# A small store of zeros goes onto the sync queue behind the first load

## The chip, the core and the metric

The kernel runs on one NeuronCore of a Trainium2 chip. The core has a matrix engine (TensorE, called PE in the profile), a vector engine (VectorE, DVE), a scalar engine (ScalarE, ACT), a general engine (GpSimd, POOL) and a sync engine (SyncE, SP) that here issues all transfers. Data lives in the off-chip memory (HBM) and is brought by DMA into the on-chip memory (SBUF), which has 128 partitions. A transfer is carried by 16 DMA engines.

The metric is the device time of one execution in microseconds (us): the median of 3 runs of the kernel before is 152.08 us, and the runs lie between 152.06 and 152.09.

## The reference

```python
B, S, D = 512, 32, 640          # x and fx: [512, 32, 640] bf16; alpha: [1] bf16

def reference(x, fx, alpha):
    return x + alpha * fx
```

So two tensors of 20.97 MB are read, one is written, and each element takes one multiplication and one addition. There is nothing to reuse.

## The kernel before

The three big tensors are seen as 128 rows of 80 x 1024 bf16 elements: one row for each SBUF partition (xv, fxv and ov, lines 59 to 61). A "column" below is a block of K = 1024 elements of every row, which is 256 KB over the 128 partitions. So x, fx and out have 80 columns each.

x is cut into three tiles (list X, line 18) of 32, 32 and 16 columns. The first of them is loaded by two transfers, of 4 columns and of 28 (X_CUTS, line 21). fx is cut into five tiles (list FX, line 19) of 16, 16, 19, 16 and 13 columns. Each x tile is overwritten in place with the result and then stored as a whole. Two x tiles and two fx tiles fit at a time (the pools "wide" and "fs", lines 66 and 67, with two buffers each), so a third load into a pool waits until the first tile has been used up: an x buffer is free when its store has landed, an fx buffer when the vector engine has read it.

Five helpers do the work: load_x (transfer on line 77), load_f (line 85), compute (one scalar_tensor_tensor on the vector engine, line 92, that computes fx * alpha + x over the columns that an fx tile and an x tile share), store (line 104) and alpha_to_lanes (lines 109 to 117). The last loads the single number alpha, spreads it over 128 partitions by a matrix product with a row of ones (line 115) and copies it to SBUF (line 117).

The order is written out by hand in the string PLAN (lines 22 to 41), and the schedule is manual: nothing reorders it. In PLAN "x 0" loads x tile 0, "f 1" loads fx tile 1, "c 2 1" computes fx tile 2 with x tile 1, "s 0" stores tile 0, and "a" fetches alpha. In the text below the transfers are called x0a (4 columns), x0b (28 columns), alpha, f0, f1, x1, f2, s0, f3, x2, f4, s1 and s2, which is the order in which SP issues them. All of them go on one queue, SP's, and SP issues strictly in this order: an instruction that waits on SP holds back all that follow. After the last store a no-op on SP waits for everything but that store (lines 126 to 129).

POOL runs nothing in this kernel apart from four small memsets of constants that the launch code puts ahead of the body (line 144).

Of the kernel before, what the change touches and what calls it, by code (L numbers as in the profile page):

```python
# [2 lines left out]

# [4 lines left out]

ACT = mybir.ActivationFunctionType
ALU = mybir.AluOpType  # L10
F32 = mybir.dt.float32
BF16 = mybir.dt.bfloat16

K = 1024
P = 128


X = [(0, 32), (32, 64), (64, 80)]
FX = [(0, 16), (16, 32), (32, 51), (51, 67), (67, 80)]

X_CUTS = {0: (4,)}
PLAN = """
x 0
a
f 0
f 1
x 1
c 0 0
f 2
c 1 0  # L30
s 0
f 3
x 2
c 2 1
f 4
c 3 1
c 3 2
s 1
c 4 2
s 2  # L40
"""


@with_exitstack
def kernel(
    ctx: ExitStack,
    tc: tile.TileContext,
    x: bass.AP,
    fx: bass.AP,
    alpha: bass.AP,  # L50
    out: bass.AP,
):

    nc = tc.nc
    xv = x.flatten_outer_dims().rearrange("(p n) d -> p (n d)", p=P)
    fxv = fx.flatten_outer_dims().rearrange("(p n) d -> p (n d)", p=P)  # L60
    ov = out.flatten_outer_dims().rearrange("(p n) d -> p (n d)", p=P)
    assert xv.shape[1] == X[-1][1] * K == FX[-1][1] * K

    consts = ctx.enter_context(tc.tile_pool(name="consts", bufs=1))
    psum = ctx.enter_context(tc.tile_pool(name="psum", bufs=1, space=bass.MemoryType.PSUM))
    wide = ctx.enter_context(tc.tile_pool(name="wide", bufs=2))
    fs = ctx.enter_context(tc.tile_pool(name="fs", bufs=2))
    ctx.enter_context(tc.manual_schedule())

    xt, ft = {}, {}  # L70
    done = []

    def load_x(i):
        a, b = X[i]
        xt[i] = wide.tile([P, max(e - s for s, e in X) * K], x.dtype, tag="x", name="x_t")
        for c, d in pairwise((a, *X_CUTS.get(i, ()), b)):
            r = nc.sync.dma_start(  # L77
                out=xt[i][:, (c - a) * K : (d - a) * K], in_=xv[:, c * K : d * K]
            )
            done.append(r)  # L80

    def load_f(j):
        a, b = FX[j]
        ft[j] = fs.tile([P, max(e - s for s, e in FX) * K], fx.dtype, tag="f", name="f_t")
        r = nc.sync.dma_start(out=ft[j][:, : (b - a) * K], in_=fxv[:, a * K : b * K])
        done.append(r)

    def compute(j, i):
        (fa, fb), (xa, xb) = FX[j], X[i]
        a, b = max(fa, xa), min(fb, xb)  # L90
        piece = xt[i][:, (a - xa) * K : (b - xa) * K]
        r = nc.vector.scalar_tensor_tensor(  # L92
            out=piece,
            in0=ft[j][:, (a - fa) * K : (b - fa) * K],
            scalar=lanes["a_f"][:],
            in1=piece,
            op0=ALU.mult,
            op1=ALU.add,
        )
        done.append(r)  # L100

    def store(i):
        a, b = X[i]
        r = nc.sync.dma_start(out=ov[:, a * K : b * K], in_=xt[i][:, : (b - a) * K])
        done.append(r)

    lanes = {}

    def alpha_to_lanes():
        a_1 = consts.tile([1, 1], alpha.dtype, name="a_1")  # L110
        done.append(nc.sync.dma_start(out=a_1[:], in_=alpha[None, :]))  # L111
        ones = consts.tile([1, P], alpha.dtype, name="ones")
        nc.vector.memset(ones[:], 1.0)  # L113
        a_ps = psum.tile([P, 1], F32, name="a_ps")
        done.append(nc.tensor.matmul(a_ps[:], ones[:], a_1[:], start=True, stop=True))  # L115
        lanes["a_f"] = consts.tile([P, 1], F32, name="a_f")
        nc.vector.tensor_copy(out=lanes["a_f"][:], in_=a_ps[:])  # L117

    does = {"x": load_x, "f": load_f, "c": compute, "s": store, "a": alpha_to_lanes}
    for step in PLAN.split("\n"):  # L120
        if step:
            what, *of = step.split()
            does[what](*map(int, of))


    rest = nc.sync.nop(nofuse=True)
    info = mybir.DependencyInfo(mybir.DependencyClass.Sync, mybir.DependencyReason.DATA)
    for i in done[:-1]:
        tc.add_manual_dep(rest.ins, i.ins.name, info, reason="all but the last store")


# [1 line left out]
_INS = ['x', 'fx', 'alpha']  # L133
_OUTS = [((512, 32, 640), 'bfloat16')]


# [23 lines left out]
```

## Time and profile before

| | |
|---|---|
| Median of 3 runs | 152.08 us (152.06 to 152.09) |
| The profiled execution: span from its first to its last instruction | 150.2 us |
| DMA share of the span (16 engines) | 98.1% |
| Bytes moved | 62.92 MB, at 419 GB/s over the span |
| Vector engine busy | 86.8 us, 58% of the span |
| Matrix engine busy | 0.2 us |
| POOL busy | 0.2 us, 4 memsets |

The profiled execution's own time is its span; no other time is given for it. The runs are 1.9 us longer than the span, which is what lies around the first and the last instruction.

How to read it. The page gives the busy time of each engine, the span in 40 slices, the DMA queues, and the chain of work that ended last, followed back from the end. A row "DMA f_t<-in_fx_dram" in this chain says that the chain ran through a transfer into an fx tile, from its issue on SP to its landing. Since transfers queue behind each other, most of such a time is spent in the queue. A list of the issues gives for each transfer its size and the time from issue to landing; where several transfers have the same size and line the median is given, and the view of one line gives the smallest, the median and the largest of its transfers. A landing is counted when the last of the 16 engines has reported.

### The profile page before, as it was taken

The numbers are of one execution on the slowest core, as the hardware profiler recorded it, in microseconds if no ns is written. First come the engines' busy times: TensorE is split into PE (matmuls) and PEld (weight loads), VectorE is DVE, ScalarE is ACT, GpSimd is POOL, SyncE is SP. The second block draws the span as 40 slices with busy tenths as digits, with TensorE's granted clock in tenths as the row PEclk, the third lists the DMA queues.
The fourth block names the chain that finished last, engine by engine and source line by source line (L and its number), as shares of the span: only waits on it lengthen the run. The fifth ranks groups of instructions, "written<-read, shape, count | busy, mean of one in ns | idle before, by whom it ended". The sixth has DMA issues, their size and how long they took to land.

```text
span 150.2 us, 78 instructions
## 1 busy us (share of the span) xinstructions
PE 0.2 (0%) x1; PEld 0.1 (0%) x1; DVE 86.8 (58%) x8; POOL 0.2 (0%) x4
## 2 busy tenths in 40 slices
PE   0000000000000000000000000000000000000000
PEld 0000000000000000000000000000000000000000
DVE  0000000049999999970399999106999999980000
POOL 0000000000000000000000000000000000000000
DMA  5997989999969696999696999999999969696994
GB/s 179 589 428 305 489 384 419 436 454 471 576 297 559 279 559 279 497 394 435 279 559 279 559 401 410 445 419 419 419 393 454 620 279 559 279 559 297 454 463 183
DMA packets 1730, 62.92 MB, mean 419 GB/s; under 512 B 194, under 2 KB 194, under 8 KB 194
## 3 DMA queue, kind: packets, MB, share of 16 engines
q1 hardware_dynamic: 1730, 62.92, 98.1%
HBM read 41.94 MB, written 20.97 MB: 419 GB/s over the span
## 4 chain that ended last, share of the span: by engine, by line
DMA 54%; DVE 35%; SPq 1%; issue 0%; DVEq 0%
DMA f_t<-in_fx_dram 54%; DVE x_t L92 35%; SPq L77 1%; SPq L111 0%; DVEq L92 0%
## 5 line engine op out<-in xcount | busy, mean ns | idle before, releaser
L92 DVE SCALAR_TENSOR_TENSOR x_t<-f_t,a_f,x_t 128x16384 bf16<-128x16384 bf16 (+3 forms) x6 | 86.5, 14438 | 25.5 <-DMA f_t<-in_fx_dram 25.5
L117 DVE COPY a_f<-a_ps 128x1 f32<-128x1 f32 x1 | 0.2, 159 | 21.5 <-PE a_ps L115 21.5
L113 DVE MEMSET ones<- 1x128 bf16 x1 | 0.2, 165 | 0.8 <-PEq L144 0.8
L115 PE MATMUL a_ps<-a,ones 1*128 1x1 bf16 x1 | 0.2, 158 | 22.2 <-DMA a<-in_alpha_dram 22.2
L144 POOL MEMSET const-bfloat16-1.0<- 128x1 bf16 x1 | 0.1, 103 | 0.0
L144 POOL MEMSET const-uint8-127<- 128x1 uint8 x1 | 0.1, 103 | 0.0
L115 PEld LDWEIGHTS <-ones 1*128 1x128 bf16 x1 | 0.1, 100 | 1.0 <-DVE ones L113 1.0
L144 POOL MEMSET const-float32-1.0<- 128x1 f32 x1 | 0.1, 100 | 0.0
L144 POOL MEMSET const-float32-0.0<- 128x1 f32 x1 | 0.1, 99 | 0.2 <-issue 0.2
## 6 DMA issues: line engine op xcount, KB each, us to landing
f_t<-in_fx_dram SPq DMA_DIRECT2D x3, 4096.0 KB, 35.6
x_t<-in_x_dram SPq DMA_DIRECT2D x1, 7168.0 KB, 21.3
f_t<-in_fx_dram SPq DMA_DIRECT2D x1, 4864.0 KB, 24.1
x_t<-in_x_dram SPq DMA_DIRECT2D x1, 4096.0 KB, 19.2
out_dram<-x_t SPq DMA_DIRECT2D x1, 4096.0 KB, 14.9
f_t<-in_fx_dram SPq DMA_DIRECT2D x1, 3328.0 KB
x_t<-in_x_dram SPq DMA_DIRECT2D x1, 1024.0 KB, 4.8
out_dram<-x_t SPq DMA_DIRECT2D x2, 24.7
```

What stands on the lines that cost most here:

```text
L77: r = nc.sync.dma_start(out=xt[i][:, (c - a) * K : (d - a) * K], in_=xv[:, c * K : d * K])
L92: r = nc.vector.scalar_tensor_tensor(out=piece, in0=ft[j][:, (a - fa) * K : (b - fa) * K], scalar=lanes["a_f"][:], in1=piece, op0=ALU.mult ...
L113: nc.vector.memset(ones[:], 1.0)
L115: done.append(nc.tensor.matmul(a_ps[:], ones[:], a_1[:], start=True, stop=True))
L117: nc.vector.tensor_copy(out=lanes["a_f"][:], in_=a_ps[:])
L144: nc = _bacc.Bacc("TRN2", target_bir_lowering=False, num_devices=1)
```

## The change

A tile named blank of 16 partitions by 512 bf16 elements (1 KiB per partition, 16 KiB in all) is set to zero by a memset on POOL at the start of the body. Right behind x0a, and ahead of x0b, SP issues a transfer that stores this tile to the first 512 elements of the first 16 rows of out. The store s0 later writes these places again with the result. s0 therefore waits for the small store too, and so does the no-op at the end, since the small store is in the list done. The wait of the small store for the memset is new on SP. On all engines the order of the other instructions is unchanged.

```diff
--- before.py
+++ after.py
@@ -18,6 +18,7 @@
 X = [(0, 32), (32, 64), (64, 80)]
 FX = [(0, 16), (16, 32), (32, 51), (51, 67), (67, 80)]
 
+HEAD = 16
 X_CUTS = {0: (4,)}
 PLAN = """
 x 0
@@ -67,6 +68,9 @@
     fs = ctx.enter_context(tc.tile_pool(name="fs", bufs=2))
     ctx.enter_context(tc.manual_schedule())
 
+    blank = consts.tile([HEAD, 512], out.dtype, name="blank")
+    nc.gpsimd.memset(blank[:], 0.0)
+
     xt, ft = {}, {}
     done = []
 
@@ -78,6 +82,8 @@
                 out=xt[i][:, (c - a) * K : (d - a) * K], in_=xv[:, c * K : d * K]
             )
             done.append(r)
+            if (i, c) == (0, 0):
+                done.append(nc.sync.dma_start(out=ov[:HEAD, :512], in_=blank[:]))
 
     def load_f(j):
         a, b = FX[j]
```

## The prediction

> **What bounds the kernel now.** I read the page's DMA part first, then the chain, then the list of issues, and last SP's own rows in the order of time. The DMA part settles who is the bound:
>
> ```profile
> span 150.2 us, 78 instructions
> q1 hardware_dynamic: 1730, 62.92, 98.1%
> HBM read 41.94 MB, written 20.97 MB: 419 GB/s over the span
> ```
>
> The 16 DMA engines are busy for 98.1% of the span, so the idle part is 1.9% of 150.2, or 2.9 us, and the start and the end take that. Any time that is won or lost is won or lost on the one queue that feeds these engines. The vector engine is busy for 58% only. The count of packets also says how a transfer is spread: 12 big transfers of 128 rows and 16 closing packets each are 12 x 144 = 1728, and alpha has 2.
>
> The question is then whether the queue runs equally fast everywhere. For that I take issue and landing times. The chain gives the landings of the fx tiles that the vector engine waited for:
>
> ```profile
> 1.16 0.42 SPq L77
> ...
> 1.99 30.16 DMA f_t<-in_fx_dram
> ...
> 49.59 24.12 DMA f_t<-in_fx_dram
> ...
> 94.31 26.12 DMA f_t<-in_fx_dram
> ```
>
> The row of L77 is SP's issue of x0b. In the DMA rows the first number is the issue, the sum is the landing: f0 lands at 32.15, f2 at 73.71, f4 at 120.43. The list of issues gives sizes and times to landing of the others, and the views of single lines give the largest and smallest of a line:
>
> ```profile
> x_t<-in_x_dram SPq DMA_DIRECT2D x1, 7168.0 KB, 21.3
> f_t<-in_fx_dram SPq DMA_DIRECT2D x1, 4864.0 KB, 24.1
> x_t<-in_x_dram SPq DMA_DIRECT2D x1, 4096.0 KB, 19.2
> x_t<-in_x_dram SPq DMA_DIRECT2D x1, 1024.0 KB, 4.8
> x_t<-in_x_dram SPq DMA_DIRECT2D x1, 58.3
> ...
> DMA to landing us min/median/max: 24.1/32.9/39.5
> ...
> DMA to landing us min/median/max: 14.9/22.8/26.6
> ```
>
> ```profile
> 0.73 0.86 SPq L77 DMA_DIRECT2D x_t<-in_x_dram  x2
> 1.63 0.32 SPq L111 DMA_DIRECT2D a<-in_alpha_dram  x1
> 1.99 0.87 SPq L85 DMA_DIRECT2D f_t<-in_fx_dram  x2
> 2.90 0.45 SPq L77 DMA_DIRECT2D x_t<-in_x_dram  x1
> 49.59 0.33 SPq L85 DMA_DIRECT2D f_t<-in_fx_dram  x1
> 66.78 0.35 SPq L104 DMA_DIRECT2D out_dram<-x_t  x1
> 67.19 0.42 SPq L85 DMA_DIRECT2D f_t<-in_fx_dram  x1
> 93.37 0.33 SPq L77 DMA_DIRECT2D x_t<-in_x_dram  x1
> ...
> 116.95 17.96 SPq L104 DMA_DIRECT2D out_dram<-x_t  x2
> ```
>
> With these, x0a lands at 0.73 + 4.8 = 5.5; x0b (issued at 1.16 by the chain) at 22.46; x1 at 2.90 + 58.3 = 61.2; s0 at 66.78 + 26.6 = 93.4; x2 at 93.37 + 19.2 = 112.57; s1, issued at 116.95, at 139.75 (the middle value, 22.8). The time from one landing to the next, per 1024 KB, is: x0b 16.9/7 = 2.42; f0 9.69/4 = 2.42; x1 (from f1, which is issued at about 2.43 and lands at 41.9) 19.3/8 = 2.41; **f2 12.51/4.75 = 2.63**; s0 19.66/8 = 2.46; f4 7.86/3.25 = 2.42; s1 19.32/8 = 2.41. So the queue runs at one steady rate, loads and stores alike, with one exception. f2, at 2.42, should take 11.50 us and takes 12.51: **1.0 us is missing**. No late issue explains it: f2 is issued at 49.59 and its place in the queue comes at 61.2. What happens during f2's turn is that SP issues the first store of the kernel, s0, at 66.78. The second store, s1, is issued at 116.95 in the middle of f4 in the same way, and f4 loses nothing (7.86 against 3.25 x 2.42 = 7.87). So the loss goes with the first store, not with stores as such.
>
> **The change part by part.** Five edits have to be priced.
>
> *The memset on POOL.* Lower end: the constants' memsets on POOL take 0.10 us each. Upper end: the vector engine's widest operation takes 20.485 us for 19456 elements a partition, 1.05 ns each, so 512 would take 0.54, with 0.10 on top 0.64 us. POOL has nothing else to do, and the body begins at about 0.8 (the first memset on DVE starts at 0.81). The zeros are there between 0.9 and 1.5 us. I take the upper end, as it is the nearer in width.
>
> *The issue on SP.* Issues take 0.32 to 0.45 us. SP is through with x0a at 1.10, then waits for the memset until 1.1 to 1.5, then issues for up to 0.45. x0b goes out at 1.5 to 2.0 instead of 1.16, and alpha, f0, f1 and x1, which are queued behind it on SP, go out 0.35 to 0.8 later. What hides this is x0a's own transfer. x0a takes 4.8 us from issue to landing, of which 2.42 are its bytes; the other 2.4 are start and close. If all of that were start, x0b would have to be issued by 5.5 - 2.4 = 3.1 us to be in the queue in time. It goes at 2.0 at the latest, so 1.1 us of cover is left and the cost is zero; without that cover each microsecond of delay would cost one. Alpha lands before 22.24 (the matmul on L115 starts then) and its result is first needed at 32.2, so its delay has 9.7 us of cover.
>
> *The bytes.* 16 KB at 2.42 us per 1024 KB are 0.04 us, plus a closing packet on each engine. Alpha's small transfer sits between x0b and f0, and f0 still shows 2.42 per 1024 KB, so a small transfer costs nothing that the landings show. I take 0.05, from 0.04 to 0.1.
>
> There is a rule that speaks against this edit: the Trainium skill, page "DMA: Bandwidth & Descriptors", section "Anatomy of one DMA — SWDGE (gpsimd) path", gives every transfer a fixed cost of about 2.0 us, most of it the wait for the write to be confirmed, and calls HBM the slowest target; the section states it for another queue than SP's. If that sat on the queue, the estimate from the page would be 152.08 + 2.0 = 154.1 us less whatever is won at f2. The closest row here is the turn from s0 to f3: f3 lands at 67.19 + 35.6 = 102.79 (35.6 is the median of f0, f1 and f3, and it is f3's), 9.4 us after s0 for 4 x 2.42 = 9.68, so f3 did not wait for s0's confirmation.
>
> *The first store is now another one.* In f2's turn the 1.0 us can go. By the landings' rounding (0.05 each) and the spread of the steady rate (2.41 to 2.44 times 4.75) the loss is 0.9 to 1.1; a landing is the last of 16 engines, and engines that came early may have lost more, so I keep 1.3 as the outer end. Below, it is 0 if the loss stays where it is. At the head the same loss may show up anew: 0 to 1.0 us. The trace has no store early on, so this is the open price. For 0: at that time the queue is still starting (2.4 us of x0a's 4.8 are not its bytes), so a delay of the first write can lie beside it; the store has one row for each of the 16 engines and 1 KiB in each, where s0 has 64 KiB rows; and all 16 are touched, so that s0 finds none for the first time. For 1.0: x0a and x0b are in flight as f2 was. I take 0, by the first ground, and keep 1.0 for the range.
>
> *The added waits.* s0 waits for the small store, which has landed some 60 us before; the no-op likewise. Both cost nothing, and would cost something only if the small store were later than 66 us. What is late next once f2 comes 1.0 us earlier? The vector engine starts f2's piece 1.0 earlier, f4's issue (94.31) and s1's (116.95) move along, and s1 is still issued 3.5 us before f4 lands, s2 (about 134.6) 5 us before s1 lands at 139.75. So the queue stays fed and all of the gain reaches the end.
>
> Sum: 0 + 0 + 0.05 - 1.0 + 0 + 0 = -0.95. Against the profiled span that is 150.2 to 149.25, and with the 1.9 us around it **151.1 us**, against the median of 152.08.
>
> **The rivals.** *The loss moves whole to the head.* If the first store stalls the queue for the same 1.0 us wherever it stands, x0b lands 1.0 later and f2 makes it good: 152.08 + 0.05 = 152.1. For it: the queue is busy in both places, and a busy queue has no gap for a stall. Against: the start is not yet at the steady rate.
>
> *The change does not do what it could: the loss is not the first store's.* f2 is also the one tile with 38 KiB rows, and f3 is issued right after s0, at 67.19. If the loss is f2's own or belongs to s0's large rows, nothing moves: again 152.1. Against: f4 has odd rows too (26 KiB) and keeps 2.42.
>
> *Slower: paid twice.* A first store stalls the queue at the head (1.0) and s0, the first large store, still stalls at f2 (1.0 as before): 152.08 + 1.0 + 0.05 = 153.1. It decides from the point where the head's stall exceeds what f2 gets back; with half a stall at the head it is 152.6. For it: the trace shows only that the second large store is free, not that a small one makes the first large one free. Against: only the argument that the small store touches all 16 engines and the same tensor.
>
> **How the numbers follow.** A measurement of this kernel can tell about 0.2%, 0.3 us, from no change. Forecast (stall gone from f2, most of it hidden at the head, 150.75 to 151.75): 0.60. Moved whole, or not the first store's at all, 152.1 for both: 0.07 and 0.06. Paid twice, 152.4 to 153.1: 0.27. Faster is the first case, same the second and third, slower the last. The range takes 150.8 (152.08 + 0.05 - 1.3) below, and above it goes to 152.8, which leaves the upper half of the slower case outside (0.13) and a few hundredths below. The forecast's own range is 150.8 to 151.75.
>
> **What would show it.** In the changed kernel's list of issues, f2's landing less x1's should be 11.5 us; if it is 12.5, the loss stayed. x0b's landing should be at 22.5 to 22.6; 23.5 says that the stall moved. SP's rows should show the small store's issue by 1.5 and x0b's by 2.0; x0b issued after 3.1 would open a gap in the first slices. The DMA share should stay at 98% or rise. Wrong I would be above all if a stall belongs to the first large write, or if the queue cannot hide a first write in its start.

## The result, and the profile after

The changed kernel takes 152.43 us (median of 20 runs, 152.03 to 153.81) against 152.06 us for the kernel before (20 runs, 151.90 to 152.25) on the same chip: a ratio of 1.0033, with an interval of 1.0018 to 1.0048. So it is slower, by 0.37 us, where 151.1 us and a gain were forecast. On two more chips it was slower by less: 152.03 against 151.95 us (1.0008, 0.9999 to 1.0017) and 152.09 against 151.95 us (1.0015, 1.0006 to 1.0024). Over the three, nothing is won, and 0.1 to 0.4 us are lost; on the second chip the interval still has room for no loss.

The profiled execution of the changed kernel took 152.44 us, with a span of 150.7 us. Its page:

```profile
span 150.7 us, 82 instructions
...
q1 hardware_dynamic: 1762, 62.93, 97.8%
HBM read 41.94 MB, written 20.99 MB: 418 GB/s over the span
...
L72 POOL MEMSET blank<- 16x512 bf16 x1 | 0.5, 514 | 0.3 <-POOLq L150 0.3
```

The packets are 32 more: 16 rows and 16 closing packets. The timeline shows what SP issues (start, time of the issue):

```profile
0.74 0.38 SPq L81 DMA_DIRECT2D x_t<-in_x_dram  x1
1.27 0.35 SPq L86 DMA_DIRECT2D out_dram<-blank  x1
1.67 0.41 SPq L81 DMA_DIRECT2D x_t<-in_x_dram  x1
2.13 0.32 SPq L117 DMA_DIRECT2D a<-in_alpha_dram  x1
2.50 0.82 SPq L91 DMA_DIRECT2D f_t<-in_fx_dram  x2
3.36 0.47 SPq L81 DMA_DIRECT2D x_t<-in_x_dram  x1
49.77 0.33 SPq L91 DMA_DIRECT2D f_t<-in_fx_dram  x1
66.97 0.34 SPq L110 DMA_DIRECT2D out_dram<-x_t  x1
67.37 0.44 SPq L91 DMA_DIRECT2D f_t<-in_fx_dram  x1
93.60 0.33 SPq L81 DMA_DIRECT2D x_t<-in_x_dram  x1
```

The list of issues (size, time from issue to landing), and the chain (issue, time to landing):

```profile
x_t<-in_x_dram SPq DMA_DIRECT2D x1, 7168.0 KB, 21.0
...
x_t<-in_x_dram SPq DMA_DIRECT2D x1, 4096.0 KB, 19.3
...
x_t<-in_x_dram SPq DMA_DIRECT2D x1, 1024.0 KB, 4.7
...
out_dram<-blank SPq DMA_DIRECT2D x1, 16.0 KB, 4.3
...
x_t<-in_x_dram SPq DMA_DIRECT2D x1, 58.0
```

```profile
2.50 29.85 DMA f_t<-in_fx_dram
...
49.77 24.44 DMA f_t<-in_fx_dram
...
94.82 26.02 DMA f_t<-in_fx_dram
```

| Landing, us | before | after | difference |
|---|---|---|---|
| x0a | 5.5 | 5.4 | |
| small store | | 5.6 | |
| x0b | 22.46 | 22.67 | 0.2 |
| f0 | 32.15 | 32.35 | 0.2 |
| x1 | 61.2 | 61.36 | 0.2 |
| f2 | 73.71 | 74.21 | 0.5 |
| f4 | 120.43 | 120.84 | 0.4 |

Two readings matter. x0b lands 0.2 us later, and f0 and x1 keep that distance. It can't be put down to the small store: over the thirteen traces of this case without a small transfer at the head, x0b lands between 22.5 and 22.8 us, and over the four with the small store between 22.6 and 22.8. Of the store's own cost the trace shows that its 16 rows took 0.046 us each. And f2 still stalls: it takes 74.21 - 61.36 = 12.85 us after x1's landing, where the steady rate gives 11.5. The stall has not gone and not moved; in this execution it is 0.3 us longer.

A shorter way to read the stall serves for the runs below. f2 is issued when the vector engine is done with f0, some 11.6 us before x1 lands, in all of these kernels. So the time from f2's issue to its landing is 11.6 plus f2's own turn: 24.12 before, 24.44 here, and about 23.15 where nothing stalls.

### The profile page after: what moved, and what is told of

The parts are those of the page before. It is cut to its first block, busy times and chain, and to the rows that moved or that the text cites. A ratio compares the mean times of both kernels' runs of the same rounds, so it can differ in the third digit from the quotient of the medians.

```text
span 150.7 us, 82 instructions
## 1 busy us (share of the span) xinstructions
PE 0.2 (0%) x1; PEld 0.1 (0%) x1; DVE 86.8 (58%) x8; POOL 0.7 (0%) x5
## 4 chain that ended last, share of the span: by engine, by line
DMA 53%; DVE 34%; SPq 1%; POOLq 0%; issue 0%; DVEq 0%
DMA f_t<-in_fx_dram 53%; DVE x_t L98 34%; POOLq L161 0%; SPq L81 0%; SPq L86 0%; SPq L117 0%; DVEq L98 0%; POOLq L150 0%
## 5 line engine op out<-in xcount | busy, mean ns | idle before, releaser
L72 POOL MEMSET blank<- 16x512 bf16 x1 | 0.5, 514 | 0.3 <-POOLq L150 0.3
## 6 DMA issues: line engine op xcount, KB each, us to landing
x_t<-in_x_dram SPq DMA_DIRECT2D x1, 4096.0 KB, 19.3
```

The lines of the kernel that those rows point to most:

```text
L72: nc.gpsimd.memset(blank[:], 0.0)
```

## The experiments

In the table, f2 is the time from its issue to its landing, in us, in the profiled execution. All ratios are against the kernel before on the same chip.

| Kernel | time, us | ratio (interval) | f2 |
|---|---|---|---|
| before, traced again | 152.02 | 1.0005 (0.9996 to 1.0015) | 24.09 |
| after, 2nd chip | 152.03 | 1.0008 (0.9999 to 1.0017) | 24.11 |
| after, 3rd chip | 152.09 | 1.0015 (1.0006 to 1.0024) | 24.12 |
| small load instead | 151.88 | 1.0003 (0.9994 to 1.0013) | 23.42 |
| small load, again | 152.04 | 1.0002 (0.9993 to 1.0011) | 23.92 |
| 128 rows | 152.09 | 1.0017 (1.0007 to 1.0027) | 23.76 |
| small store behind x1 | 152.04 | 1.0008 (0.9999 to 1.0017) | 24.21 |
| s0 made a load | 151.09 | 0.9948 (0.9930 to 0.9966) | 23.17 |
| f3 later | 151.96 | 1.0000 (0.9992 to 1.0009) | 23.92 |
| s0 later | 151.66 | 0.9976 (0.9967 to 0.9985) | 23.16 |
| s0 later, again | 151.38 | 0.9959 (0.9945 to 0.9974) | 23.15 |
| after, s0 later | 151.92 | 0.9996 (0.9984 to 1.0007) | 23.14 |
| s1 early | 152.08 | 1.0010 (1.0001 to 1.0019) | 23.94 |
| s0 a load, s1 early | 151.51 | 0.9972 (0.9962 to 0.9982) | 23.16 |
| s0 later, s1 early | 152.05 | 1.0007 (0.9995 to 1.0018) | 23.15 |
| s0 and s1 later | 151.37 | 0.9958 (0.9946 to 0.9970) | 23.1 |
| s0 and s1 later, again | 151.23 | 0.9942 (0.9929 to 0.9956) | 23.2 |
| s0 in halves | 152.42 | 1.0027 (1.0011 to 1.0043) | (order differs) |

**Is the loss the store's, or that of anything at this place?** The small transfer is turned round.

```diff
-                done.append(nc.sync.dma_start(out=ov[:HEAD, :512], in_=blank[:]))
+                done.append(nc.sync.dma_start(out=blank[:], in_=xv[:HEAD, :512]))
```

> The changed kernel with the small transfer turned round: it loads 16 rows of 1 KiB of x into the tile blank, at the same place behind x0a and with the same wait for the memset; s0 no longer waits for it. Nothing but the direction and that wait differs. Theory A, the write to HBM at the head does the harm (a cost to the 16 engines that only a store has): the loss goes, 152.05 to 152.15 us. Theory B, any small transfer between x0a and x0b sets the 16 engines apart, or the later issue of x0b does it: 152.3 to 152.5 us, as with the store. In both f2 takes about 12.5 us from x1's landing, since the first store is s0.

Measured: 151.88 us, ratio 1.0003: no loss, as theory A has it, though on this chip the store itself loses only 0.14 us (the changed kernel on the 3rd chip), so this run alone does not decide between A and B. And f2 took 23.42 us in the profiled execution, less than any kernel with s0 as it was, which nobody had expected; the run was made once more further down.

**Were 16 rows too few?**

```diff
-HEAD = 16
+HEAD = 128
```

> The changed kernel with 128 rows of 1 KiB instead of 16, so that the small store touches every row of out, 8 on each engine. Theory C, the stall in f2's turn is a first touch of the rows of out, and 16 rows were too few: f2 takes 11.5 us from x1's landing instead of 12.5 to 12.9, and the kernel runs at 151.2 to 151.6 us, as 128 KB cost 0.3 us. Theory D, the stall belongs to the first store with large rows or to f2 itself: f2 stays at 12.5 or above and the time is 152.4 to 153.0 us.

Measured: 152.09 us, slower by 0.17%; f2 took 23.76 us. The stall is smaller in this execution (0.6 us above 23.15 instead of 0.95) but there. That the 128 rows made it smaller is not shown, since it was smaller still (0.3 us) with the small load, which touches no row of out. Theory C is out: every row of out had been touched, and s0 still stalled f2.

**Is it the place at the head?** The small store is issued behind x1, where it waits 57.9 us for its turn.

```diff
-            if (i, c) == (0, 0):
-                done.append(nc.sync.dma_start(out=ov[:HEAD, :512], in_=blank[:]))
+        if i == 1:
+            done.append(nc.sync.dma_start(out=ov[:HEAD, :512], in_=blank[:]))
```

> The small store of 16 rows goes out behind x1, the last of the first loads, instead of behind x0a; x0b is issued as early as in the kernel before. It is carried at about 61 us, between x1 and f2. If the place at the head does the harm (the engines are still getting up to speed there), the loss goes: 152.1 us. If any small store ahead of s0 does it, 152.4 us with a wide spread remains. If the first store stalls the queue wherever it stands and only its nearness to s0 was missing, f2 changes: the stall would fall into x1's last packets and f2 would take 11.5 us.

Measured: 152.04 us, ratio 1.0008, and f2 at 24.21 us. The store took nothing from the stall here either, and did not stall x1 (x1 lands at 3.12 + 58.2 = 61.3 us, as before). So a 16 KB store is no stand-in for s0 at either of the two places tried.

**Does the stall need the store s0 at all?** s0 is replaced by a load of the same size, and the kernel leaves out the first 32 columns of the output.

```diff
+        if i == 0:
+            r = nc.sync.dma_start(out=xt[i][:, : (b - a) * K], in_=xv[:, a * K : b * K])
+        else:
+            r = nc.sync.dma_start(out=ov[:, a * K : b * K], in_=xt[i][:, : (b - a) * K])
-        r = nc.sync.dma_start(out=ov[:, a * K : b * K], in_=xt[i][:, : (b - a) * K])
```

> The kernel before, with the first store s0 replaced by a load of the same size at the same place (the first 32 columns of x are loaded into x tile 0 again); the first 32 columns of the output are left out. The first store is now s1, issued in f4's turn. If the stall belongs to the first store, f2 takes 11.5 us from x1's landing, and f4 takes 8.9 us from x2's landing instead of 7.86. If it belongs to f2 (38 KiB rows) or to the issues at 67 us, f2 stays at 12.5 us and f4 at 7.86.

Measured: 151.09 us (2 runs), ratio 0.9948. Its chain shows f2 and f4:

```profile
49.79 23.17 DMA f_t<-in_fx_dram
...
93.57 26.09 DMA f_t<-in_fx_dram
```

f2 falls from 24.12 to 23.17: the stall is gone, so it does come from a store behind f2, not from f2's 38 KiB rows or from the time of 67 us. The 0.84 us (151.93 - 151.09) is about what the stall is worth. But f4, with s1 behind it as the first store, takes what it did before: x2 lands at 92.32 + 19.4 = 111.72, f4 at 119.66, 7.94 us against 7.86. "The first store" alone is then not the rule.

**The same two kernels on another chip.**

> The kernel before, unchanged, for a trace of it from the same chip as the changed kernel's and the next two. From x1's landing to f2's it should take 12.3 to 12.7 us, 1 us above the steady 11.5, if the stall is a property of the kernel and not of one execution.

> The changed kernel, unchanged, beside the kernel before on this chip. If the loss is the kernel's own, it is slower by 0.2 to 0.5 us with a wider spread; the trace should show x0b's landing some 0.15 to 0.25 us later than before and f2 taking 12.3 to 12.9 us from x1's landing. If the loss belonged to the first chip, the two agree within 0.1 us.

Measured: f2 takes 24.09 us in the kernel before and 24.11 in the changed one, so the stall is a property of both, and of one size. x0b lands at 22.47 and 22.57 us. The changed kernel is 0.08 us slower, at the edge of what can be told.

**Is it the load f3 queued behind s0?** f3's issue also waits for f2's landing.

```diff
+        got[j] = r
+        if j == 3:
+            tc.add_manual_dep(r.ins, got[2].ins.name, info, reason="f3 after f2 has landed")
```

> The kernel before, with one more wait: the issue of f3, right behind s0 on SP, also waits until f2 has landed (about 72 to 73 us instead of 67). f3 is carried after s0, so from 92 us on, and the queue does not run dry. Theory E, the stall comes from a store that stands in the queue with a load behind it (s1 and s2 have none and cause no stall): f2 takes 11.5 us and the kernel 151.0 to 151.2 us. Theory F, the stall is s0's own (its rows, its time of issue, the 38 KiB rows ahead of it): f2 stays at 12.3 to 12.7 us and the time at that of the kernel before.

Measured: f3 is issued at 73.77 us, f2 takes 23.92, the time is 151.96 us, ratio 1.0000. Theory E falls: with nothing queued behind s0, f2 stalls nearly as before.

**Is it how long s0 waits in the queue?** The vector engine, idle from 67 to 74 us, first runs one operation of 2560 columns on the spent f1 tile, and s0 waits for it. s0 is issued at 69.8 us instead of 66.8.

```diff
+        if (j, i) == (1, 0):
+            last[0] = nc.vector.scalar_tensor_tensor(
+                out=ft[1][:, :2560], in0=ft[1][:, :2560], scalar=lanes["a_f"][:],
+                in1=ft[1][:, :2560], op0=ALU.mult, op1=ALU.add)
...
+        if i == 0:
+            tc.add_manual_dep(r.ins, last[0].ins.name, info, reason="s0 goes out later")
```

> The kernel before, with s0 and f3 issued about 2.8 us later, at 69.6 instead of 66.8: the vector engine, idle there, first runs one operation of 2560 columns on the spent f1 tile. s0 then has to wait in the queue for 2.3 us instead of 5.1, about as s1 does behind f4 (2.6). Theory G, the stall arises when a store stands in the queue for long behind loads, or when it comes while several of f2's rows are outstanding: f2 takes 11.5 us, the kernel 151.0 to 151.2 us. If it is tied to s0 as such, f2 stays at 12.3 to 12.7 us; if the stall follows the issue by a fixed time of some 3.5 us, it falls into s0's first rows instead and the total is unchanged.

> The kernel before with s0 and f3 issued about 2.8 us later, as in the run of that kind before, again beside the next three. If a store stalls the loads ahead of it when it is issued long before its turn (here 2.3 us ahead instead of 5.1), f2 takes 11.5 us from x1's landing and the time is 151.4 to 151.8 us.

Measured: f2 takes 23.16 and 23.15 us, the time is 151.66 (ratio 0.9976) and on another chip 151.38 us (0.9959). The same store of the same rows at the same place does not stall the loads ahead of it when it is issued 3.0 us before f2 lands (69.86 to 72.90) instead of 6.9 (66.78 to 73.71). The waits below are counted in this way, from a store's issue to the landing of the load ahead of it; the expectations count to the moment when the store's first rows should start, and so give less (2.3 and 5.1 here). SP's issue of s0 and the chain in the second of these runs:

```profile
69.86 0.35 SPq L121 DMA_DIRECT2D out_dram<-x_t  x1
...
49.75 23.15 DMA f_t<-in_fx_dram
...
93.50 26.72 DMA f_t<-in_fx_dram
```

But the full 0.84 us is not won, since f4 is now late: x2 lands at 92.64 + 19.4 = 112.04 us, f4 at 120.22, which is 8.2 us (and 8.6 in the first run) instead of 7.9, as if a part of the stall had passed to f4, ahead of the second store. Both traces are of the slowest execution of their kernel (151.91 and 151.79 us), so they may show more of this than the median has.

A part of it also falls into s0's own turn, which the landings hide. By the single packets in the traces, 12 to 14 of s0's 128 rows, begun at 88.6 to 89.5 us, are stretched in every kernel with the late s0, the longest to 2.8 to 3.0 us where the others take 2.42. Added up and divided by the 16 engines this is 0.2 us, against 0.8 to 1.3 us in f2's rows in the kernel before and the changed one. In the kernel before no row of s0 is stretched. So the late issue makes the stall much smaller and moves what is left; it does not remove all of it.

Two things besides the issue of s0 differ here. f3 is issued later too, but in the run before this one a later f3 alone left the stall nearly whole. And the vector engine does one more operation; no run has that operation without the wait. Two of the kernels with s1 issued early, further down, do without it.

**The change with the late s0.** The same delay in the changed kernel.

> The changed kernel, small store included, with s0 and f3 issued about 2.8 us later in the same way. The loss of the change may sit in two places: at the head (the small store's bytes and what it does to the start) or in a longer stall in f2's turn. If it is at the head alone, this kernel is slower than the one without the small store (same delay of s0) by the same 0.1 to 0.4 us, and x0b lands later by that much. If it is in f2's stall, the two agree within 0.1 us, since the stall is gone in both.

Measured: 151.92 us, ratio 0.9996, with f2 at 23.14 us and f4 at 8.45 (x2 lands at 92.68 + 19.3 = 111.98, f4 at 120.43). With f2's stall out of the way the small store still costs: 151.92 against 151.38 us beside it (151.66 for that kernel on the other chip), and x0b lands at 22.77 against 22.6 us. So the loss does not need a longer stall in f2. Where it sits this pair does not show: x0b's 22.77 us lie within what the kernels without the small store have, and f4 is late in both.

**Does s1 stall f4 when it waits long?** fx is cut at 64 columns instead of 67, so that s1 is issued at 115.0 us, some 5 us before f4's landing.

```diff
-FX = [(0, 16), (16, 32), (32, 51), (51, 67), (67, 80)]
+FX = [(0, 16), (16, 32), (32, 51), (51, 64), (64, 80)]
...
-c 3 2
```

> The kernel before with fx cut at 64 columns instead of 67 (f3 has 13 columns, f4 has 16, and one operation of the vector engine goes). s1 is then issued some 1.8 us earlier while f4's turn ends when it did, so s1 waits about 4.7 us in the queue instead of 2.8. If a store that waits long in the queue stalls the loads ahead of it, f4 (16 columns, 9.68 us at the steady rate) takes 10.3 to 10.9 us, and the kernel 152.5 to 153.0 us. If the stall is s0's alone, f4 takes 9.7 us and the time stays at 151.9 to 152.1.

> s0 is replaced by a load of the same size (the first 32 columns of the output are left out) and fx is cut at 64 columns, so that s1 is the first store and is issued some 4.5 us before its turn behind f4 (16 columns, 9.68 us at the steady rate). If the stall belongs to the first large store that waits long in the queue, f4 takes 10.5 us or more; if it belongs to s0 itself, f4 takes 9.7 us and no transfer shows a stall: 151.0 to 151.2 us.

> s0 and f3 are issued 2.8 us later, so that s0 waits 2.3 us in the queue, and fx is cut at 64 columns, so that s1 waits some 4.4 us. f2 should take 11.5 us as before with the late s0. If the stall falls to the first store that waits long, f4 now takes 10.5 us or more, where it showed 0.1 to 0.2 us on a few engines with the early s0: 152.0 us or more. If s0's stall is its own, f4 takes 9.7 to 9.9 us: 151.3 to 151.7 us.

The three belong together; f4 has 16 columns in each, 9.68 us at the steady rate. With s0 as before, which stalls f2 (23.94), f4 takes 9.71 us: x2 lands at 93.22 + 17.4 = 110.62, f4 at 120.33. With s0 made a load, so that s1 is the first store, f4 takes 10.0 us: 92.23 + 17.6 = 109.83 to 119.82. With s0 late, f4 takes 10.3 us: 92.75 + 17.4 = 110.15 to 120.43. From s1's issue to f4's landing it is 5.3, 5.6 and 5.9 us. The issue of s1 (the row covers s1 and s2) and f4 in the first two, s0 as before and s0 as a load:

```profile
115.04 23.14 SPq L103 DMA_DIRECT2D out_dram<-x_t  x2
...
94.20 26.13 DMA f_t<-in_fx_dram
```

```profile
114.25 23.41 SPq L106 DMA_DIRECT2D out_dram<-x_t  x2
...
93.47 26.35 DMA f_t<-in_fx_dram
```

The chain of the last:

```profile
49.92 23.15 DMA f_t<-in_fx_dram
...
93.68 26.75 DMA f_t<-in_fx_dram
```

A long wait alone does not stall (the first of the three), and being the first alone does not either (s0 made a load, with s1 issued 3.5 us before f4's landing, 116.16 to 119.66). It is the first store that waits long: where s0 did not pay, s1 pays, 0.3 and 0.6 us. This is less than the 0.8 us that were expected of it, so the rule has the right direction and an open size. In time, 151.51 against 151.09 us for the two kernels with s0 as a load on the same chip (ratios 0.9972 and 0.9948) says the same; some 0.1 us of it may be the other cut of fx, which with s0 as before takes 152.08 against 151.98 us.

**Shorter waits for both stores.** s0 is issued 2.8 us later, and s1 1 us later, by one more operation, of 900 columns.

```diff
+LATER = {(1, 0): 2560, (3, 1): 900}
...
+        if (j, i) in LATER:
+            last[i] = idle(j, LATER[j, i])
...
+        if i in last:
+            tc.add_manual_dep(r.ins, last[i].ins.name, info, reason="goes out later")
```

Here idle(j, columns) is the vector engine's operation on the first columns of the spent fx tile j, as above.

> The kernel before with s0 and f3 issued 2.8 us later and s1 issued about 1 us later (one more operation of 900 columns on the vector engine behind f3's piece). s1 then waits 1.8 us in the queue instead of 2.8. If the stall depends on how long the store waits in the queue, f2 and f4 both run at the steady rate on all engines: 151.0 to 151.3 us, with a narrow spread. If the late stall of single engines in f4 has another cause, the time stays at 151.4 to 151.8.

> The kernel before with s0 and f3 issued 2.8 us later and s1 1 us later, again on another chip: 151.2 to 151.5 us against about 151.95, f2 at 11.5 us from x1's landing and f4 at 7.9 from x2's.

Measured: 151.37 us (151.22 to 151.50), ratio 0.9958, and on another chip 151.23 us (151.11 to 151.31), ratio 0.9942: faster than both kernels of this case, with a narrow spread. s1 lands at 117.51 + 21.6 = 139.1 us in the second run, against 116.52 + 23.1 = 139.6 with the late s0 alone, so its later issue does not make it late. The stretched rows at the end of s0 are still there. The timeline of the second run shows the late stores (SP's issues; the last row covers s1 and s2):

```profile
69.96 0.35 SPq L121 DMA_DIRECT2D out_dram<-x_t  x1
70.36 0.42 SPq L100 DMA_DIRECT2D f_t<-in_fx_dram  x1
92.50 0.33 SPq L92 DMA_DIRECT2D x_t<-in_x_dram  x1
93.60 0.33 SPq L100 DMA_DIRECT2D f_t<-in_fx_dram  x1
117.51 17.67 SPq L121 DMA_DIRECT2D out_dram<-x_t  x2
```

**The small store against the small load, on one chip.**

> The changed kernel on another chip. Slower than the kernel before by 0.05 us (its bytes alone) to 0.4 us (what the first chip showed). f2 takes 12.3 to 12.9 us from x1's landing.

> The changed kernel with a small load in place of the small store, beside it on the same chip. In its first trace f2 took 11.9 us (landing of the slowest engine) and x0b landed 0.2 us later. If a small load at the head really shortens the stall, f2 takes 11.7 to 12.0 us again and the time is 0.1 to 0.4 us below that of the small store; if that was one execution's chance, f2 takes 12.3 to 12.9 and the two agree within 0.1 us.

Measured: the store 152.09 us (1.0015), the load 152.04 us (1.0002), f2 at 24.12 and 23.92. The short stall with the small load did not come back; it varies from execution to execution there (23.42, 23.92). The load is not slower than the kernel before in either run; the two kernels differ by 0.05 us in the medians, which is too little to say that the direction matters.

**Can a large early store take the stall with it?** s0 goes out in halves. The first half is stored as soon as it is computed, ahead of f2, and stands in the queue behind x1.

```diff
 c 0 0
+s 0 0 16
 f 2
 c 1 0
-s 0
+s 0 16 32
```

> The kernel before with s0 in two halves of 16 columns: the first goes out as soon as its 16 columns are computed (49.6 us), ahead of f2, and stands in the queue behind x1; the second follows f2 as s0 did. The bytes and the output are the same. If the stall goes with the first large store that waits long in the queue, x1 takes 0.8 to 1.3 us longer than its 19.3 us and f2 takes 11.5 us (counted from the landing of the first half): the stall has moved, and the time is that of the kernel before within 0.3 us. If the stall belongs to the place behind f2 (38 KiB rows, the time of 67 us), x1 keeps 19.3 us and f2 takes 12.3 us or more.

SP's issue of the first half, and the list of issues, which has x1 in the row without a size, and the halves and s2 in the row of three:

```profile
49.67 0.35 SPq L106 DMA_DIRECT2D out_dram<-x_t  x1
...
out_dram<-x_t SPq DMA_DIRECT2D x3, 4096.0 KB, 22.6
...
x_t<-in_x_dram SPq DMA_DIRECT2D x1, 59.2
```

and the chain has f2:

```profile
50.07 33.37 DMA f_t<-in_fx_dram
```

x1, issued at 2.96 us, now takes 59.2 us to land instead of 58.3: 0.9 us longer, at 62.2. The first half lands at 49.67 + 22.6 = 72.3, f2 at 83.44, 11.2 us later; behind a store the steady rate gives 11.5 less the 0.3 by which stores land late (as f3 behind s0 before), so f2 is free of the stall, though the second half waits behind it for 16.6 us (66.87 to 83.44). The stall has moved with the first large store that waits. The time, 152.42 us (ratio 1.0027, 152.02 to 153.38), is a little above that of the kernel before, with a wide spread like that of the changed kernel on the first chip; the trace is of an execution of 152.09 us and does not show where the spread comes from.

## Why the prediction was wrong

**The bound, and the stall in f2's turn: right.** The one queue sets the time, and the time missing from f2 is a stall that a store makes: without it the kernel takes 0.84 us less, with 1.0 put on it. Two readings there are loose and change nothing: no row gives the 2.44 at the upper end of the steady rate, and s0's 2.46 was passed over, by which s0 lands 0.3 us late and f3 after it takes 0.3 us less.

**The memset and the issues: right.** The memset took 0.51 us (0.10 to 0.64, taken at the upper end), the small store was issued at 1.27 and x0b at 1.67 us (at most 2.0 was said), and the queue did not run dry: x0a's transfer covered it.

**The bytes: right, as far as the traces can tell.** 0.05 us was put on them, and the store's rows took 0.046 us each. x0b's landing was later by 0.2 us on the first chip and by 0.1 on the second and third (22.57 and 1.69 + 20.9 = 22.59 against 22.46), which is no more than it varies without the small store (22.5 to 22.8). The rule of the Trainium skill that was weighed (page "DMA: Bandwidth & Descriptors", section "Anatomy of one DMA — SWDGE (gpsimd) path", about 2.0 us for each transfer) would have given far too much on this queue: the whole change cost 0.1 to 0.4 us. The small store itself took 4.3 us from issue to landing, but the loads behind it did not wait for that.

**"The first store is now another one": wrong, and this is the step that failed.** The 1.0 us at f2 was to go because all 16 engines had made a store before. The runs showed in its place that the stall goes with the first large store that stands in the queue for long behind loads: it was paid with waits of 5.6 us and more, and hardly or not at all with 3.0 and 3.5 us. A 16 KB store does not take it over: f2 took 24.44 us with it at the head (24.12 before) and 24.21 with it behind x1. With 128 KB f2 took 23.76 us in one execution, still 0.6 above 23.15; the first half of s0 (4096 KB) took it over, and x1 paid 0.9 us. The argument that a store touching all 16 engines was as good as s0 had no row behind it, and two grounds that spoke against it stood in the text: s0 has rows of 64 KiB and the small one of 1 KiB, and "paid twice" said that the trace did not show a small store making the first large one free. The head's own share was rightly taken as 0: no stall of that size showed there.

**The second store as proof that it is the first: half right.** f4 was not stalled by s1 in the kernel before, and that was read as "the second is free". In the kernel with s0 as a load s1 was the first and f4 was still free, when s1 waits for 3.5 us only; issued earlier, with 5.6 us, it cost 0.3 us. The prediction compared two stores that differ in two things, order and waiting time, and named one.

**The rivals.** Nearest was the second, that the stall belongs to s0's large rows and nothing moves, at 152.1 us and with a chance of 0.06. "Paid twice" did not happen: nothing stalled at the head. What the loss of 0.37 us on the first chip is made of, beyond some 0.05 us of bytes, is not settled. In the profiled execution it lies in f2's turn (0.3), but on the other two chips f2's turn was not longer than before, and with the late s0 the loss was there without it.

What stays open as well is why the stall arises. The traces show its conditions, not its cause, and the conditions are not complete: with the late s0, s1 cost f4 0.3 to 0.7 us at waits of 3.7 to 4.2 us, the stall included, and as the first store, with s0 a load, it cost next to nothing at 3.5 us.

## What to carry to other kernels

Read one queue's transfers as rate per byte from landing to landing: a single slow transfer in an even row says more than the busy share. Before a stall is put down to "the first of its kind", look for the other things in which the first differs from the second, here how long it stood in the queue, and try the cheap one: issuing s0 3 us later and s1 1 us later won 0.4 to 0.6%, where the early store won nothing. A stand-in that is to take over a one-time cost has to be like the original in size, not only in kind: here 16 KB and 128 KB were too little and 4096 KB was enough.

## What the runs showed of the hardware that was not expected

A large store that was issued 6.9 us before the landing of the load ahead of it slowed that load on the same queue by about 1 us (f2 at 24.1 instead of 23.15 us), and the same store issued 3.0 us before that landing did not. The Trainium skill, page "DMA: Bandwidth & Descriptors", section "Queues, rings and completion order", says that each engine consumes a queue's descriptors in ring order. The order alone does not keep the loads ahead free: a store behind f2 slowed it in these runs. Only the first such store did so: after it, s1 with a wait of some 5 us cost f4 0.03 us. With s0 late, a part of the stall turned up ahead of s1 (f4 at 8.2 to 8.6 us instead of 7.9), as if it were put off and not removed, until s1 was issued later too; another part stayed in s0's last rows (0.2 us for each engine on average).
